# Two queues for q's weights, bias loads further back, w2 in three loads

## The chip, the cores and the metric

The kernel runs on one core of one Trainium2 chip. The metric is the device time of one execution in microseconds (us); for the comparison several executions are timed and their median is taken. Engines go by these names: PE is TensorE's matmul, PEld its weight load, DVE is VectorE, ACT ScalarE, POOL GpSimd, SP SyncE. A "q" behind a name (SPq, ACTq) is the part of that engine that issues DMAs.

## The reference, cut to what matters

The program normalizes x (2048 rows of 640, bf16), feeds the result into an attention branch and an MLP branch, and adds both to x.

```python
def _A_ref(x, wqkv, wo):                 # H = 32 heads, W = 8 taps, dilation 2
    qkv = (x @ wqkv).reshape(B, S, 3, H, Dh)...
    q, k, v = qkv[0], qkv[1], qkv[2]
    idx = pos[:, None] - off[None, :]    # each row sees itself and 7 earlier rows, 2 apart
    logits = jnp.einsum("bhsd,bhswd->bhsw", q, kg) * scale     # idx < 0 masked
    o = jnp.einsum("bhsw,bhswd->bhsd", softmax(logits), vg)
    return o.reshape(B, S, D) @ wo

def _B_ref(x, w1, b1, w2, b2):           # F = 1536
    return gelu(x @ w1 + b1) @ w2 + b2

x = A_x
xn = _layernorm(x, axis=-1)
return x + _A_ref(xn, A_wqkv, A_wo) + _B_ref(xn, B_w1, B_b1, B_w2, B_b2)
```

## The kernel before, in words

The 2048 rows are worked on in four chunks of 512 rows, each of four blocks of 128 rows. x lies in SBUF as `x_sb`, 16 blocks wide; the weights lie there whole, with the 640 input channels in five tiles of 128 (`KT`): `wq_sb`, `wk_sb`, `wv_sb`, `w_sb` (w1, and also w2) and `wo`.

Before the main part the loads are issued in the order of the source (lines 131 to 142), as far as each one's own inputs are ready. On SyncE: x block 0 (L126), q's weights (`load_w(0)`, L129), x blocks 2 and 3, k's weights, x blocks 4 to 7, v's weights, and w1 in two loads (L142). On ScalarE: x block 1 (L132), and the two biases into `b_rt`, 12 rows of b1 (L133) and 5 rows of b2 (L134). Block 1's load waits for a small GpSimd memset in `x_sb` (L120), and the bias loads for one in `b_rt` (L121). The loads share a small set of completion counters, taken in turn, so a later load waits until an earlier one that used the same counter has landed; L142 does so.

Everything behind that runs in an order that is written out by hand, the long string `ORDER`: each name stands for a piece of work, and every engine works through its own instructions in that order. These names matter here:

- `st00` (L213, L215) are block 0's mean and variance on VectorE, `sum1`, `neg1` and `sq1` (L225, L229, L232) those of block 1 on ScalarE, `rs00` and `rs01` (L244, L247) the reciprocal deviations of the two blocks on ScalarE.
- `xn00a`, `xn00b`, `xn01b`, `xn01a` (L264) normalize on VectorE, `tp...` (L279) transpose on TensorE into PSUM, `tc...` (L284) copy the result to `xnT`.
- `ga`, `gb2` to `gb4` (L346) are q's 25 matmuls for block 0, by input tile: `ga` takes tiles 0 and 1, `gb2` tile 2, `gb3` and `gb4` tiles 3 and 4. `gd` and `ge` do the same for block 1. `hj...` (L377) are the q, k and v matmuls of the rest of chunk 0.
- `tb` (L453) is one small matmul that transposes the 17 bias rows, and `b1` (L456) copies them to `bT`, which the first GELU reads (L627).
- `wa`, `wb` and the matmuls at L443 in front of the string work on constants alone and write to a bank that nothing reads.
- `qk0...` (L430) are the products of q and k on VectorE. `f1` (L611) is the first MLP product, `t...` (L690) the second with the attention's output product; they read w1 and w2. `ld2` (L153) loads w2, in four loads.

The first names of the string give the order at the start:

```python
pad01 pad02 st00a st00 sum1 rs00 neg1 xn00a sq1 xn00b tp00a wa tp00b tc00a wb rs01 tc00b ga xn01b gb2 xn01a tp01b
st03a tp01a tb tc01b gb3 tc01a gb4 st03 gd gc0 st02a ge rs03 st02 hj101 xn03 rs02 gc1 xn02 tp03 gc4 st12a tp02 tc03
```

Of the kernel before, what the change touches and what calls it, by code (L numbers as in the profile page):

```python
# [16 lines left out]
S, D, F, H, W, DIL = 2048, 640, 1536, 32, 8, 2  # L17
P = 128
DH = D // H
PAD = (W - 1) * DIL  # L20
KT, FT = D // P, F // P
# [17 lines left out]

ORDER = """  # L40
pad01 pad02 st00a st00 sum1 rs00 neg1 xn00a sq1 xn00b tp00a wa tp00b tc00a wb rs01 tc00b ga xn01b gb2 xn01a tp01b
st03a tp01a tb tc01b gb3 tc01a gb4 st03 gd gc0 st02a ge rs03 st02 hj101 xn03 rs02 gc1 xn02 tp03 gc4 st12a tp02 tc03
hj100 st13a st13 tc02 st12 hj102 hc101 st11a hj111 hc100 st10a hc102 st11 hj010 st10 hc111 ho b1 rs1 hj112 pk rc1 qk01
hj110 xn13 hc112 hj012 tc13 xn11 hj200 hc010 hc110 tc11 qk00 hj011 hc200 hc012 hj201 hc011 xn10 f10_1 hc201 qk02 tc10
xn12 f10_11 tc12 f10_2 ldx ge0_1 f10_5 qk03 ge0_11 ge0_2 f10_3 ge0_5 f10_0 pad11 ge0_3 pa00 pj103 ge0_0 pj100 pc103
pa01 su20 xp2 pj110 pc100 ld2 pj101 pc110 su22 pb01 pj104 su21 pj102 pc101 su23 pb04 pj114 pc104 ng2 pc102 pj112 ldo
# [27 lines left out]
def kernel(  # L74
# [16 lines left out]
    nc = tc.nc  # L91
# [23 lines left out]
    wqkv = [wts.tile([P, KT, D], BF16, name=f"w{s}_sb") for s in "qkv"]  # L115
# [3 lines left out]
    b_rt = consts.tile([P, P], BF16, name="b_rt")  # L119
    nc.gpsimd.memset(x_sb[:, 1, 0:16], 0.0)  # L120
    nc.gpsimd.memset(b_rt[:], 0.0)  # L121
    wqkv_v = A_wqkv.rearrange("(t p) n -> p t n", p=P)
    w1_v = B_w1.rearrange("(t p) n -> p t n", p=P)

    def load_x(b0, b1):
        nc.sync.dma_start(x_sb[:, b0:b1, :], x_nb[:, b0:b1, :])  # L126

    def load_w(s):
        nc.sync.dma_start(wqkv[s][:], wqkv_v[:, :, s * D : (s + 1) * D])  # L129

    load_x(0, 1)
    nc.scalar.dma_start(x_sb[:, 1, :], x_nb[:, 1, :])  # L132
    nc.scalar.dma_start(b_rt[0:FT, :], B_b1.rearrange("(t p) -> t p", p=P))  # L133
    nc.scalar.dma_start(b_rt[FT : FT + KT, :], B_b2.rearrange("(t p) -> t p", p=P))  # L134
    load_w(0)
    load_x(2, BPC)
    load_w(1)
    load_x(BPC, 2 * BPC)
    load_w(2)
    for c in range(2):  # L140
        cs = slice(c * F // 2, (c + 1) * F // 2)
        nc.sync.dma_start(w1_sb[:, :, cs], w1_v[:, :, cs])  # L142
# [5 lines left out]

    def do_ld2():
        w2_v = B_w2.rearrange("(t p) n -> p t n", p=P)  # L150
        for c in range(4):
            ts = slice(c * FT // 4, (c + 1) * FT // 4)
            nc.sync.dma_start(w2_sb[:, ts, :], w2_v[:, ts, :])  # L153

    def do_ldo():
# [695 lines left out]
```

## Time and profile before

| | |
|---|---|
| median of 3 runs | 205.5 us (205.43 to 206.93) |
| profiled execution | 205.49 us |
| its span in the trace | 203.3 us |
| TensorE busy | 199.4 us, 98% of the span |
| VectorE busy | 185.8 us, 91% |
| ScalarE busy | 129.7 us, 64% |
| moved by DMA | 27.31 MB |

The span is the stretch that the trace covers; the profiled execution's own time is 2.19 us longer. Rows of the timeline give start, length, engine, line, operation, output and inputs, and in brackets how long the engine stood idle ahead of it and what ended that. Rows of the chain give start, length and what it was. Rows of the DMA issues give what was loaded, who issued it, how often, the size of one and the median time from issue to landing. Rows of windows give the stretch, its length, the busy time (and instructions) of PE, PEld, DVE, ACT and POOL, TensorE's granted clock, the share of the DMA engines that was busy, and GB/s. Rows of queues give packets, MB and share; q1 carries SyncE's loads, and q10 those of ScalarE.

### The profile page before, as it was taken

What the parts mean: (1) busy time and instruction counts of PE and PEld (TensorE: products, weight loads), DVE (VectorE), ACT (ScalarE), POOL (GpSimd) and SP (SyncE); (2) the same over time, 40 slices, a digit from 0 to 9 for tenths busy, and PEclk for the clock granted to TensorE, in tenths of its full rate; (3) what the DMA queues carried; (4) which work ended last, traced back from release to release, by engine and by line L of the source; (5) the groups of instructions that cost most, each with busy time, mean ns of one, the idle gap of its engine ahead of it and who ended that gap; (6) DMA issues with size and microseconds to landing.
All of it is one profiled execution on the core that took longest, in us unless ns stands there. A gap on an engine that the chain in (4) does not pass through costs nothing.

```text
span 203.3 us, 2874 instructions
## 1 busy us (share of the span) xinstructions
PE 199.4 (98%) x1100; PEld 105.0 (52%) x1100; DVE 185.8 (91%) x159; ACT 129.7 (64%) x237; POOL 29.5 (14%) x35
## 2 busy tenths in 40 slices
PE   8999999999999999999999999999999999999994
PEld 3899455654454555444444544444444445444552
DVE  2899999899997999999999996999979999999981
ACT  5689979999979897555545437697447990211100
POOL 3000000000000400024202500000202702253420
PEclk9999999999999999999999999999999999999999
DMA  6996399940673681849912890001863898895951
GB/s 204 390 395 208 77 355 336 348 148 3 91 155 89 110 148 22 219 92 163 193 17 52 102 99 5 3 0 15 170 98 69 153 118 147 111 120 90 103 90 64
DMA packets 38430, 27.31 MB, mean 134 GB/s; under 512 B 25106, under 2 KB 34578, under 8 KB 38418
## 3 DMA queue, kind: packets, MB, share of 16 engines
q1 hardware_dynamic: 28016, 20.29, 38.2%
q0 software_dynamic: 10080, 6.56, 26.3%
q10 hardware_dynamic: 322, 0.30, 0.4%
q8 instruction: 8, 0.13, 0.3%
q14 instruction: 4, 0.03, 0.0%
HBM read 10.49 MB, written 4.59 MB: 74 GB/s over the span
## 4 chain that ended last, share of the span: by engine, by line
PE 96%; DMA 2%; SPq 0%; DVE 0%; issue 0%
PE T L690 27%; PE hps L611 25%; PE pps L333 24%; PE lo L646 7%; PE gps L377 7%; DMA wq_sb<-in_A_wqkv_dram 2%; PE hi L646 2%; PE gps L346 1%; PE L L480 1%; PE tp L279 0%; SPq L126 0%; DVE prod L658 0%; PE tb L453 0%
## 5 line engine op out<-in xcount | busy, mean ns | idle before, releaser
L611 PE MATMUL hps<-xnT,w_sb 128*128 128x512 bf16 x240 | 56.9, 379 | 0.0
L430 DVE TENSOR_TENSOR prod<-qT,kT 128x5120 bf16<-128x5120 bf16 x16 | 44.5, 2820 | 0.1
L690 PE MATMUL T<-hT,w_sb 128*128 128x512 bf16 x180 | 43.4, 379 | 0.0
L611 PEld LDWEIGHTS <-w_sb 128*128 128x128 bf16 x240 | 23.5, 98 | 27.5
L702 POOL DMA_DIRECT2D out_dram<-x_sb x15 | 20.9, 1492 | 87.5 <-DMA x_sb<-x_sb 87.5
L627 ACT ACTIVATE hT<-hps,bT 128x512 bf16<-128x512 f32 x36 | 23.9, 689 | 12.1 <-PE hps L611 9.6
L690 PEld LDWEIGHTS <-w_sb 128*128 128x128 bf16 x180 | 17.5, 98 | 21.1 <-issue 0.4
L693 ACT ACTIVATE x_sb<-T,bT 128x512 bf16<-128x512 f32 x15 | 10.3, 688 | 25.6 <-PE T L690 24.5
L581 DVE TENSOR_TENSOR prod<-vT,ax 128x5120 bf16<-128x5120 bf16 x8 | 22.4, 2820 | 2.7 <-PE L L480 1.5
L581 DVE TENSOR_TENSOR prod<-vT,x_sb 128x5120 bf16<-128x5120 bf16 x8 | 22.2, 2817 | 0.0
L592 POOL DMA_DIRECT2D prod<-prod x6 | 7.8, 1300 | 77.5 <-DVE prod L581 77.5
L170 ACT ACT_TABLE_LOAD x14 | 18.0, 1283 | 1.0 <-PEq L835 0.7
L471 DVE TENSOR_TENSOR prod<-prod 128x4096 bf16<-128x4096 bf16 x8 | 18.3, 2291 | 0.3
L333 PE MATMUL pps<-xnT,wv_sb 128*128 128x512 bf16 x75 | 18.5, 379 | 0.0
L690 PE MATMUL T<-oT,wo 128*128 128x512 bf16 x75 | 18.5, 379 | 0.0
L333 PE MATMUL pps<-xnT,wq_sb 128*128 128x512 bf16 x75 | 18.1, 379 | 0.0
L465 DVE TENSOR_TENSOR prod<-prod 128x4096 bf16<-128x4096 bf16 x8 | 18.0, 2286 | 0.0
L333 PE MATMUL pps<-xnT,wk_sb 128*128 128x512 bf16 x75 | 18.0, 380 | 0.0
L594 DVE TENSOR_TENSOR prod<-prod 128x2560 bf16<-128x2560 bf16 x10 | 14.8, 1487 | 0.1
L333 PEld LDWEIGHTS <-wq_sb 128*128 128x128 bf16 x75 | 8.8, 117 | 7.5
L333 PEld LDWEIGHTS <-wv_sb 128*128 128x128 bf16 x75 | 8.7, 118 | 7.6 <-issue 0.4
L333 PEld LDWEIGHTS <-wk_sb 128*128 128x128 bf16 x75 | 8.6, 118 | 7.7 <-issue 0.8
(91 smaller groups left out, 242.6 us busy)
## 6 DMA issues: line engine op xcount, KB each, us to landing
prod<-prod POOLq DMA_DIRECT2D x6, 640.0 KB, 6.8
ax<-attn SPq DMA_DIRECT2D x8, 256.0 KB, 3.9
x_sb<-attn SPq DMA_DIRECT2D x8, 256.0 KB, 4.5
w_sb<-in_B_w_dram SPq DMA_DIRECT2D x2, 960.0 KB, 11.0
out_dram<-x_sb SPq DMA_DIRECT2D x3, 640.0 KB, 6.8
w_sb<-in_B_w_dram SPq DMA_DIRECT2D x4, 480.0 KB, 6.6
out_dram<-x_sb POOLq DMA_DIRECT2D x15, 128.0 KB, 5.6
x_sb<-in_A_x_dram SPq DMA_DIRECT2D x2, 640.0 KB, 7.0
```

The lines of the kernel that those rows point to most:

```text
L170: nc.scalar.preload_act_table_set(name)
L333: nc.tensor.matmul(ps[:], lhsT=wqkv_p[which][:, ti, to, :], rhs=xnT[:, ti, :], start=(ti == 0), stop=(ti == KT - 1),)
L430: nc.vector.tensor_tensor(out=prod[:, j], in0=q[:, :, at].unsqueeze(1).to_broadcast([P, W, KT, P]), in1=window(k, at), op=ALU.mult,)
L465: nc.vector.tensor_tensor(out=low, in0=low, in1=high, op=ALU.add)
L471: nc.vector.tensor_tensor(out=first, in0=first, in1=rows[:, :, t * P : (t + 1) * P], op=ALU.add)
L581: nc.vector.tensor_tensor(out=prod[:, j], in0=window(qkv_tile(n, 2), slice(j * P, (j + 1) * P)), in1=ax_view(n)[:, j, :, :].unsqueeze(2).t ...
L594: nc.vector.tensor_tensor(out=low, in0=low, in1=high, op=ALU.add)
L611: nc.tensor.matmul(ps[:], lhsT=w1_sb[:, ti, ft * P : (ft + 1) * P], rhs=tiles["xnT", n][:, ti, :], start=(ti == 0), stop=(ti == KT - 1),)
L627: nc.scalar.activation(hT, tiles["hps", n, ft][:], ACT.Gelu_apprx_tanh, bias=bT[:, ft : ft + 1], scale=1.0)
L646: nc.tensor.matmul(out_ps(bl, hi), lhsT=lhs, rhs=rhs[:, CH:D] if hi else rhs[:, 0:CH], start=pc == 0 and k == 0, stop=pc == 4 and k == len ...
L690: nc.tensor.matmul(ps[:], lhsT=lhs, rhs=rhs, start=pc == 0 and k == 0, stop=pc == 4 and k == len(srcs) - 1)
L702: nc.gpsimd.dma_start(dst, src, accum_op=ALU.add)
```

## The change

q's weights are loaded in two pieces: input tiles 0 to 2 by SyncE, in the place of the whole load, and tiles 3 and 4 by ScalarE. The two bias loads go from ScalarE to SyncE, behind v's weights and ahead of w1. In the order by hand, `tb` goes from the start to a place ahead of `b1`. w2 is loaded in three loads of four tiles in place of four loads of three.

```diff
 ORDER = """
...
-st03a tp01a tb tc01b gb3 tc01a gb4 st03 gd gc0 st02a ge rs03 st02 hj101 xn03 rs02 gc1 xn02 tp03 gc4 st12a tp02 tc03
-hj100 st13a st13 tc02 st12 hj102 hc101 st11a hj111 hc100 st10a hc102 st11 hj010 st10 hc111 ho b1 rs1 hj112 pk rc1 qk01
+st03a tp01a tc01b gb3 tc01a gb4 st03 gd gc0 st02a ge rs03 st02 hj101 xn03 rs02 gc1 xn02 tp03 gc4 st12a tp02 tc03 hj100
+st13a st13 tc02 st12 hj102 hc101 st11a hj111 hc100 st10a hc102 st11 hj010 st10 hc111 ho tb b1 rs1 hj112 pk rc1 qk01
...
     load_x(0, 1)
     nc.scalar.dma_start(x_sb[:, 1, :], x_nb[:, 1, :])
-    nc.scalar.dma_start(b_rt[0:FT, :], B_b1.rearrange("(t p) -> t p", p=P))
-    nc.scalar.dma_start(b_rt[FT : FT + KT, :], B_b2.rearrange("(t p) -> t p", p=P))
-    load_w(0)
+    for queue, a, b in ((nc.sync, 0, 3), (nc.scalar, 3, KT)):
+        queue.dma_start(wqkv[0][:, a:b, :], wqkv_v[:, a:b, 0:D])
     load_x(2, BPC)
     load_w(1)
     load_x(BPC, 2 * BPC)
     load_w(2)
+    nc.sync.dma_start(b_rt[0:FT, :], B_b1.rearrange("(t p) -> t p", p=P))
+    nc.sync.dma_start(b_rt[FT : FT + KT, :], B_b2.rearrange("(t p) -> t p", p=P))
...
     def do_ld2():
         w2_v = B_w2.rearrange("(t p) n -> p t n", p=P)
-        for c in range(4):
-            ts = slice(c * FT // 4, (c + 1) * FT // 4)
+        for c in range(3):
+            ts = slice(c * FT // 3, (c + 1) * FT // 3)
             nc.sync.dma_start(w2_sb[:, ts, :], w2_v[:, ts, :])
```

In the built program before, ScalarE starts with a table load (L170), then issues block 1's load, b1 and b2. In the built program after, it issues the piece of q's weights first, then block 1's load, and then comes the table load.

## Prediction

> **What bounds the kernel now.** I read the busy table first, then the chain that ended last, cut to the first 14 us (the change acts there), then the timeline of those microseconds, and last the DMA queues in small windows.
>
> ```profile
> PE 199.4 (98%) x1100; PEld 105.0 (52%) x1100; DVE 185.8 (91%) x159; ACT 129.7 (64%) x237; POOL 29.5 (14%) x35
> PE 96%; DMA 2%; SPq 0%; DVE 0%; issue 0%
> 6.30:20.00 13.70, 13.69 (x157) 13.58 (x158) 12.44 (x29) 10.91 (x27) 0.00 (x0) 1.00 0.94 334
> 1.19 5.07 DMA wq_sb<-in_A_wqkv_dram
> 6.27 0.05 issue
> 6.31 1.03 PE gps L346 x15
> ```
>
> TensorE is busy for 98% and carries 96% of the chain; from 6.3 to 20 us it works 13.69 of 13.70 us, and the chain that leads into it is q's weights, landing at 1.19 + 5.07 = 6.26 us. So TensorE in program order is the bound, with no holes behind the start: any later start of the first q matmul (L346, 6.31 us) goes into the end one to one, and any earlier start can help only as far as that matmul's other inputs allow. Those come from this chain on ScalarE and VectorE:
>
> ```profile
> 0.88 0.38 ACTq L132 DMA_DIRECT2D x_sb<-in_A_x_dram  x1
> 3.65 0.74 ACT L225 ACTIVATE trash<-x_sb 128x640 bf16<-128x640 bf16 x1 [1.63 <-DMA x_sb<-in_A_x_dram]
> 4.50 0.29 ACT L244 ACTIVATE logv<-mv,eps_t 128x1 f32<-128x1 f32 x1
> 4.83 0.20 ACT L247 ACTIVATE rstd<-logv 128x1 f32<-128x1 f32 x1
> 5.07 0.63 DVE L264 TENSOR_SCALAR xn<-x_sb,mv,rstd 128x256 bf16<-128x256 bf16 x2 [0.66 <-ACT rstd L247]
> 5.47 0.28 PE L279 MATMUL tp<-ident,xn 128*128 128x128 bf16 x2 [0.26 <-DVE xn L264]
> 5.79 0.70 DVE L284 COPY xnT<-tp 128x256 bf16<-128x256 bf16 x2
> 6.67 0.64 DVE L264 TENSOR_SCALAR xn<-x_sb,neg,rstd 128x384 bf16<-128x384 bf16 x2 [0.18 <-ACT rstd L247]
> 7.18 0.47 PE L279 MATMUL tp<-ident,xn 128*128 128x128 bf16 x5
> ```
>
> ScalarE works in program order: sum1 of block 1 (L225) stands ahead of rs00 (L244, L247), the rstd of block 0. So block 1's load (L132, landed 0.88 + 2.7 = 3.58) holds block 0's normalization too, and then every step to the first q matmul. The first of the two copies at 5.79 (0.70 for both) ends near 6.14: xnT is ready 0.17 us ahead of the matmul at 6.31. That 0.17 is all that faster weights could bring.
>
> **The change part by part.** *q's weights.* In the instruction order of the built kernel ScalarE's queue issues the two-tile piece of q first and block 1's load second, because that load waits for a memset of x_sb (L120) and the weights wait for nothing; the table load comes third. So the change doesn't only split a load: it puts 2 x 128 x 1280 B = 328 KB in front of the 164 KB that the chain above waits for. Is a queue served in order, and how do two queues share?
>
> ```profile
> wq_sb<-in_A_wqkv_dram SPq DMA_DIRECT2D x1, 800.0 KB, 5.1
> x_sb<-in_A_x_dram SPq DMA_DIRECT2D x1, 320.0 KB, 5.4
> wk_sb<-in_A_wqkv_dram SPq DMA_DIRECT2D x1, 800.0 KB, 7.0
> x_sb<-in_A_x_dram SPq DMA_DIRECT2D x1, 640.0 KB, 8.1
> wv_sb<-in_A_wqkv_dram SPq DMA_DIRECT2D x1, 800.0 KB, 9.3
> q1 hardware_dynamic: 144, 0.16, 59.4%
> q10 hardware_dynamic: 143, 0.16, 45.3%
> 0.00:3.00 3.00, 2.22 (x6) 0.87 (x7) 0.00 (x0) 1.28 (x1) 1.53 (x13) 1.00 0.38 109
> 3.00:4.10 1.10, 1.10 (x4) 0.32 (x3) 0.83 (x2) 0.45 (x1) 0.00 (x0) 1.00 0.92 297
> 4.10:4.94 0.84, 0.84 (x5) 0.37 (x4) 0.27 (x2) 0.78 (x5) 0.00 (x0) 1.00 1.06 392
> 4.94:5.37 0.43, 0.27 (x4) 0.09 (x2) 0.30 (x2) 0.40 (x3) 0.00 (x0) 1.00 1.07 393
> ```
>
> The first five rows are times from issue to landing; with the issues of SyncE (1.19, 1.66, 2.23, 2.74, 3.65 us) they land at 6.26, 7.06, 9.23, 10.84 and 12.95, in the order of issue. The next two are packets of SyncE's queue (q1) and ScalarE's (q10) from 2.3 to 3.3 us, while both had work: 144 against 143, equal shares. The last four give bytes: 3.00 x 109 + 1.10 x 297 = 654 KB moved by 4.10 us, 983 KB by 4.94, 1152 KB by 5.37.
>
> q's weights whole need x block 0, block 1 and all of q: 164 + 164 + 819 = 1147 KB, moved by 5.37, landed by 6.26, 0.89 later. After the change the same 1147 KB stand in front of SyncE's last q byte, now on two queues: its three tiles land at about 6.26 again. Gain nothing, at most the 0.17.
>
> Block 1's load: with equal shares ScalarE's queue has moved its 328 + 164 = 492 KB when SyncE's has moved 492 KB too, 984 KB in all: 4.94 us by the table. From the last byte to the landing it is 0.58 (block 1 now: 328 KB with block 0 at 3.00, landed 3.58) to 0.89 (q), so 5.5 to 5.8; but the table holds a dip (297 GB/s from 3.00 to 4.10, in which ScalarE's queue moved the small bias rows) that goes with the change, and at 392 those 1.1 us would be 0.27 shorter: 5.25 to 5.55. I take 5.35, nearer the row of this same load. Bounds: at the earliest ScalarE's queue is served first and block 0 beside it, 656 KB: 4.10 less the dip's 0.27 and plus 0.58 gives 4.4; at the latest SyncE's is served 5 to 3, 984 + 328 = 1312 KB: 4.94 + 328/393 = 5.77, plus 0.7 gives 6.47.
>
> So sum1 starts at 5.42 in place of 3.65, and rs00, the transposes, rs01 and block 1's xn all move with it by 1.77. The first q matmul could start at 6.14 + 1.77 = 7.91, against 6.31: 1.60 late. Its successors agree: block 1's xn (6.67) moves by 1.77 to end its first part near 8.75, where TensorE is done with the 15 matmuls (7.91 + 0.87). What TensorE loses there is given back nowhere, since the 13.69 of 13.70 us behind it are its own work. Bounds by the same step: 4.4 gives 0.65 late, 6.47 gives 2.7.
>
> A rule of the Trainium skill bears on the aim of the edit. "DMA: Bandwidth & Descriptors", section "Issuing engines are not separate DMA queues", says that loads issued by different engines run on the same 16 DMA engines and interleave, so that a second issuer saves only the issuing time. By it the split would be worth 0 and not even the 0.17; the 144 against 143 packets agree.
>
> *Bias loads behind v's weights, tb moved.* SyncE's two bias issues (0.64 and 0.27 us where ScalarE makes them now) come between v's issue, which ends at 4.50, and w1's first, which waits for q until 6.28 as now.
>
> ```profile
> 1.31 0.64 ACTq L133 DMA_DIRECT2D b_rt<-in_B_b_dram  x1
> 1.98 0.27 ACTq L134 DMA_DIRECT2D b_rt<-in_B_b_dram  x1
> 6.28 2.23 SPq L142 DMA_DIRECT2D w_sb<-in_B_w_dram  x2
> 7.65 0.01 PE tb L453
> 13.86 1.26 PE L377 MATMUL gps<-xnT,wq_sb 128*128 128x256 bf16 x10
> 15.05 0.17 DVE L456 COPY bT<-tb 128x17 f32<-128x17 f32 x1
> 20.49 3.83 PE L611 MATMUL hps<-xnT,w_sb 128*128 128x512 bf16 x17
> ```
>
> The biases now land just behind v, near 13.0. tb stands behind the ten matmuls of 13.86, at about 14.95 now and 16.5 after: 3.5 us of cover, cost 0 (it takes 0.01 of the chain in either place). Without the cover TensorE would stand at tb, and behind VectorE's b1 (L456) wait the first four q k products. w1 keeps its issue time and lands by about 18.7 (6.7 + 12.0, the larger of its two landings), against 20.49 + 1.6: more cover than now. Should the bias issues push it by all 0.91, it is still 19.6. Range of this part 0 to 0.
>
> *w2 in three loads.* One issue fewer, so the landings that later loads wait for keep their places.
>
> ```profile
> 28.27 3.12 SPq L153 DMA_DIRECT2D w_sb<-in_B_w_dram  x4
> w_sb<-in_B_w_dram SPq DMA_DIRECT2D x4, 480.0 KB, 6.6
> 50.82 1.29 PE T L690 x6
> ```
>
> All issued by 31.39, landed by about 38, first used at 50.82: 12 us of cover, cost 0; a third larger piece adds perhaps 2 us to a landing.
>
> **Sum.** The profiled execution took 205.49 us (span 203.3, 2.19 around it); the median of the runs shown is 205.5, so no correction. 205.49 + 1.60 = **207.1**. Own range, from landings between 4.6 and 5.95 us: 206.3 to 207.7.
>
> **The rivals.** *ScalarE's queue is served first.* For it: in its busiest part that queue took nearly all of the rate, and SyncE's second load was slow to begin; against it the equal count over the whole microsecond. It gives 205.49 + 0.65 = 206.1.
>
> *SyncE's queue gets more*, 5 to 3 as in the bound: 205.49 + 2.7 = 208.2. For it: SyncE has more and earlier issues; against it the same count.
>
> *TensorE runs slow again.* Its first matmuls ran at half the later rate:
>
> ```profile
> 0.78 4.43 PE L443 MATMUL idle<-const-bfloat16-1.0 128*128 128x512 bf16 x13 [0.78 <-PEq L835]
> 25.83 1.29 PE hps L611 x6
> ```
>
> Ten of 512 and three of 128 columns took 4.43 us; at 1.29/6 = 0.215 us for 512 they would take 2.3. The change opens a hole from 5.21, where these end, to the transposes at 5.47 + 1.77 = 7.24, and only eight small matmuls up to 7.91. If TensorE falls back and repeats the slow stretch, that is another 2.1 us: 209.2. Against it: in this trace it never falls back, though with no hole over 0.3 us to try it. The granted clock reads 1.00 in the slow stretch too, so that column can't show it. The Trainium skill, "TensorE: Matmul & The Clock Gate", section "What's actually happening", has the array fall to half after an idle window of about 3.4 us; by it a hole of 2.0 us is too short, though the few matmuls behind it leave some doubt, and no run here shows it.
>
> *Not slower.* Block 1's load isn't held by the weights in front of it, because the early rate (109 GB/s over the first 3 us) has room that a second full queue fills. The point from which it decides: a landing by 3.73 us; then the first q matmul starts when xnT is ready, 0.17 earlier than now, 205.3. Against it: 656 KB would have to be moved by 3.15 us, where the chip had moved 327 KB by 3.00 with both queues at work. This is also the case in which the change would do what it says.
>
> **How the numbers follow.** Forecast 0.57; ScalarE first 0.13; SyncE more 0.10; slow TensorE 0.12; not slower 0.05; a gain that I don't see 0.03. A measurement of this kernel can tell about 1%, 2.06 us, from no change: the limit is 207.56. Slower: 0.12 + 0.10 + the upper sixth of the forecast (0.09) = 0.31; within: 0.48 + 0.13 + 0.05 = 0.66; faster 0.03. The range 205.9 to 208.2 leaves out slow TensorE, not slower and the gain: 0.20.
>
> **What would show it.** Right: block 1's load lands at 4.6 to 5.95 us, sum1 starts just behind it, the first q matmul at 7.2 to 8.5 waits for xnT and no longer for wq_sb; SyncE's q tiles land near 6.3; TensorE has a hole from 5.2 us; tb near 16.5 with no wait; from the first k matmul on everything is later by one constant. Wrong: a first q matmul that waits for wq_sb still, block 1 landed before 4.4, six 512-column matmuls that take more than 1.29 us after the hole, or TensorE idle at tb.

## The result, and the profile after

| | median of runs | lowest to highest | ratio to before |
|---|---|---|---|
| before | 205.63 us | 205.22 to 208.37 | |
| changed | 208.48 us | 207.02 to 210.16 | 1.0114, 95% interval 1.0078 to 1.0151 |

The changed kernel is slower by 1.1%. Its six runs fall into groups by the clock that TensorE was granted: 207.02 and 207.19 us at a mean clock of 1.00, 208.48, 208.48 and 208.60 at 0.991 to 0.992, and 210.16 at 0.984. The last is the profiled execution (span 208.1 us), so this trace holds both losses in their largest form. One run of the first group alone would have looked like the forecast. Ratios leave out a run that is over 1.5% above the fastest of its kernel, so a median may move by more than its ratio.

First the page of the changed kernel: busy time by engine, granted clock in 40 slices of 5.2 us, and the chain that ended last.

```profile
PE 201.3 (97%) x1100; PEld 107.5 (52%) x1100; DVE 185.9 (89%) x159; ACT 129.7 (62%) x237; POOL 29.5 (14%) x35
...
PEclk9669999999999999999999999999999999999999
...
PE 95%; DMA 2%; issue 0%; DVE 0%; ACT 0%; POOL 0%; POOLq 0%
```

TensorE has 1.9 us more busy time for the same 1100 instructions, and the clock row shows where: second and third slice, nowhere else. Now the timeline of the first 20 us (issues of ScalarE's queue, then ScalarE, then TensorE).

```profile
0.74 0.46 ACTq L134 DMA_DIRECT2D wq_sb<-in_A_wqkv_dram  x1
1.24 0.48 ACTq L132 DMA_DIRECT2D x_sb<-in_A_x_dram  x1
...
6.38 0.74 ACT L226 ACTIVATE trash<-x_sb 128x640 bf16<-128x640 bf16 x1 [3.34 <-DMA x_sb<-in_A_x_dram]
...
8.06 0.39 PE L280 MATMUL tp<-ident,xn 128*128 128x128 bf16 x2 [3.31 <-DVE xn L265]
...
8.89 1.81 PE L347 MATMUL gps<-xnT,wq_sb 128*128 128x128 bf16 x15
...
11.02 3.57 PE L347 MATMUL gps<-xnT,wq_sb 128*128 128x128 bf16 x35
14.43 1.25 PE L378 MATMUL gps<-xnT,wk_sb 128*128 128x256 bf16 x10
...
19.90 0.17 PE L454 MATMUL tb<-ident,b_rt 128*128 128x17 bf16 x1
```

The piece of q is issued at 0.74, block 1 at 1.24, behind it. sum1 starts at 6.38, where it started at 3.65 before, and waits 3.34 us for block 1 alone. Everything behind it is late: TensorE's transposes come after a hole of 3.31 us, the first q matmul stands at 8.89 (6.31 before), and what it waits for is xn, not the weights. That is 2.58 us. Then the q matmuls themselves: 15 take 1.81 us and 35 take 3.57, against 1.03 and 2.13 before. The rows of before that follow the first 15:

```profile
7.51 2.13 PE L346 MATMUL gps<-xnT,wq_sb 128*128 128x128 bf16 x35
9.48 1.25 PE L377 MATMUL gps<-xnT,wk_sb 128*128 128x256 bf16 x10
```

Windows of the trace of the changed kernel (columns as before: stretch, length, busy time of PE, PEld, DVE, ACT and POOL, granted clock, DMA share, GB/s):

```profile
7.27:14.03 6.76, 5.97 (x57) 5.92 (x58) 4.86 (x15) 3.79 (x13) 0.00 (x0) 0.50 1.06 396
14.03:20.00 5.97, 5.97 (x66) 5.95 (x65) 4.24 (x14) 4.37 (x11) 0.00 (x0) 1.00 0.56 209
20.00:200.00 180.00, 180.00 (x929) 91.07 (x928) 172.40 (x122) 119.40 (x212) 27.94 (x22) 1.00 0.61 115
```

All through these 6.76 us the granted clock is 0.50, and behind them it is 1.00. From 20 us on TensorE is busy without a gap, 180.00 of 180.00 us. From the first q matmul to the first k matmul it takes 5.54 us (8.89 to 14.43); in a run that starts late and whose clock held it takes 3.31 (shown below), and before it took 3.17 (6.31 to 9.48). Against the run with 3.31, 2.58 us from a late start and 2.23 from the clock make 4.81, and the span grew by 208.1 - 203.3 = 4.8. The 0.14 us between 3.17 and 3.31 stands in neither term and about as much is made up later: in the run with 3.31 the first w1 matmul starts 1.74 us later than before, the last matmuls 1.63 later. So the two terms hold the difference to within some 0.15 us, and the experiments take them apart.

### The profile page after: what moved, and what is told of

Its sections match the earlier page's. It is cut to its first block, busy times and chain, and to the rows that moved or that the text cites. A ratio compares the mean times of both kernels' runs of the same rounds, so it can differ in the third digit from the quotient of the medians.

```text
span 208.1 us, 2873 instructions
## 1 busy us (share of the span) xinstructions
PE 201.3 (97%) x1100; PEld 107.5 (52%) x1100; DVE 185.9 (89%) x159; ACT 129.7 (62%) x237; POOL 29.5 (14%) x35
## 4 chain that ended last, share of the span: by engine, by line
PE 95%; DMA 2%; issue 0%; DVE 0%; ACT 0%; POOL 0%; POOLq 0%
PE T L691 26%; PE hps L612 25%; PE pps L334 24%; PE lo L647 7%; PE gps L378 7%; DMA x_sb<-in_A_x_dram 2%; PE gps L347 2%; PE hi L647 2%; PE L L481 1%; PE tp L280 1%; DVE xn L265 0%; PE idle L444 0%; DVE prod L659 0%; ACT rstd L248 0%; ACT trash L226 0%
```

## The experiments

The theory: block 1's load stands behind q's piece in ScalarE's queue, so TensorE starts late; the hole that this opens then makes the clock fall. The rivals: the two queues slow each other whatever the order; the bias loads or w2 cost something; the fall has nothing to do with the hole.

### The split kept, block 1 issued first

```diff
+    nc.gpsimd.memset(wqkv[0][:, 3, 0:16], 0.0)
```

With a memset of its own to wait for, q's piece is issued behind block 1.

> The changed kernel, but ScalarE's piece of q's weights waits for a memset behind the one that x block 1's load waits for, so block 1's load is issued first and the piece second; the split into two queues, the bias loads, tb and w2 stay as changed. Theory (the loss comes from block 1's load standing behind the weights in ScalarE's queue): block 1 lands near 3.6 us again, the first q matmul at 6.1 to 6.4, no hole in TensorE over 0.5 us, span 203.1 to 203.5, time 205.3 to 205.7. Rival (two queues for q's weights cost by themselves, since both pieces are later): the first q matmul waits for wq_sb and starts at 7 us or later, 206.2 or more.

Measured: 205.64 us, ratio 1.0007 [0.9987, 1.0028], no run with a fallen clock among 12. Its timeline:

```profile
0.88 0.38 ACTq L133 DMA_DIRECT2D x_sb<-in_A_x_dram  x1
1.30 0.45 ACTq L135 DMA_DIRECT2D wq_sb<-in_A_wqkv_dram  x1
...
3.78 0.74 ACT L227 ACTIVATE trash<-x_sb 128x640 bf16<-128x640 bf16 x1 [1.76 <-DMA x_sb<-in_A_x_dram]
...
6.55 1.07 PE L348 MATMUL gps<-xnT,wq_sb 128*128 128x128 bf16 x15
```

The whole loss is gone with the order of two issues. The first q matmul is at 6.55, a little later than I expected; its weight load waits 0.17 us for wq_sb, as the one before waited 0.28, so the split didn't bring q's weights earlier. So two queues do no harm by themselves, and bring no earlier start either: block 1 lands in time, and the first q matmul comes no sooner.

### q's weights whole, bias loads and w2 as changed

```diff
-    for queue, a, b in ((nc.sync, 0, 3), (nc.scalar, 3, KT)):
-        queue.dma_start(wqkv[0][:, a:b, :], wqkv_v[:, a:b, 0:D])
+    load_w(0)
```

> The bias loads on SyncE behind v's weights, tb moved, w2 in three loads; q's weights whole on SyncE as before. Theory: nothing, 205.3 to 205.7, first q matmul at 6.3. Rival (tb or w1 waits now): TensorE idle ahead of tb or of the first w1 matmul, 206 or more.

Measured: 205.34 us, 0.9996 [0.9983, 1.0010], first q matmul at 6.29 us. The other two edits cost nothing that can be measured.

### The hole filled: too much, then as needed

```diff
-WARM = 10
+WARM = 20      (first try)
+WARM = 15      (second try)
```

WARM sets how many 512-column matmuls on constants TensorE does ahead of the first transposes. They fill the hole and leave all else as changed.

> The changed kernel with 20 in place of 10 constant matmuls of 512 columns at the start, so that TensorE is busy to about 7.2 us. Theory (two losses: the late start, and a clock that falls to half after the hole): the late start stays, the granted clock reads 1.00 from 6 to 20 us in every run, every run ends near 207.1 (span 205.0 to 205.7), and the runs at 208.5 and above vanish. Rival (all of the loss is late data): the spread of 207.0 to 210.2 stays. Second rival (the added matmuls are themselves in the way): 207.5 or more in all runs, with the first transposes waiting for TensorE.

Measured with 20: 207.30 us (207.07 to 207.53), 1.0080 [1.0067, 1.0093], the clock 1.0 in all six runs. But the filler ran to 8.14 us and so stood in the way of the transposes, whose xn was ready near 7.3: a clean test of the clock, not of the late start. So a second try was sized to end where they begin.

> The changed kernel with 15 in place of 10 constant matmuls, so that TensorE is busy to about 6.9 us, just ahead of the transposes. Theory (late start plus a clock that falls in the hole): no run with a granted clock under 0.997, all runs at 206.7 to 207.3, and no later than with 20 matmuls, which ended at 8.1 us and stood 0.8 us in the way of the transposes. Rival (20 matmuls were needed because the clock looks back over the whole stretch up to 8 us): some runs at 208.4 or above again.

Measured with 15: 207.05 us (206.96 to 207.24), 1.0061 [1.0035, 1.0086], the clock at least 0.999 in all 12 runs. Its timeline:

```profile
0.78 6.05 PE L444 MATMUL idle<-const-bfloat16-1.0 128*128 128x512 bf16 x18 [0.78 <-PEq L836]
5.60 0.74 ACT L226 ACTIVATE trash<-x_sb 128x640 bf16<-128x640 bf16 x1 [2.56 <-DMA x_sb<-in_A_x_dram]
...
7.29 0.28 PE L280 MATMUL tp<-ident,xn 128*128 128x128 bf16 x2 [0.46 <-DVE xn L265]
...
7.95 1.00 PE L347 MATMUL gps<-xnT,wq_sb 128*128 128x128 bf16 x15
...
9.30 2.12 PE L347 MATMUL gps<-xnT,wq_sb 128*128 128x128 bf16 x35
11.26 1.26 PE L378 MATMUL gps<-xnT,wk_sb 128*128 128x256 bf16 x10
```

The start is as late as the change makes it (7.95, 1.64 late), and its span of 204.9 us is 1.6 over that of before: here is the first loss alone, 1:1. From the first q matmul to the first k matmul it takes 3.31 us. With the hole down to 0.46 us the clock held in every run, with 20 matmuls too (0 of 18 runs in all), while it fell in 9 of 12 runs of the changed kernel. So in this kernel the second loss hangs on the hole.

### The changed kernel again

No edit; the same kernel measured a second time, beside the fillers.

> The changed kernel once more, for the spread of its runs. Theory: three groups, one clock window of half speed apart: near 207.1 with a granted clock of 1.00, near 208.5 with 0.992, near 210.1 with 0.984. Rival (one broad spread of late data): times between the groups, with no tie to the granted clock.

Measured: 208.45 us, 1.0109 [1.0066, 1.0152]; one run of 207.21 at clock 1.00, five from 208.07 to 208.58 at 0.991 to 0.992, and none of the third group this time. The profiled one took 208.55. Timeline and windows:

```profile
5.78 0.74 ACT L226 ACTIVATE trash<-x_sb 128x640 bf16<-128x640 bf16 x1 [2.74 <-DMA x_sb<-in_A_x_dram]
6.51 0.28 ACT L245 ACTIVATE logv<-mv,eps_t 128x1 f32<-128x1 f32 x1
...
7.46 0.28 PE L280 MATMUL tp<-ident,xn 128*128 128x128 bf16 x2 [2.01 <-DVE xn L265]
...
8.13 1.31 PE L347 MATMUL gps<-xnT,wq_sb 128*128 128x128 bf16 x15
...
9.77 3.22 PE L347 MATMUL gps<-xnT,wq_sb 128*128 128x128 bf16 x35
12.82 1.25 PE L378 MATMUL gps<-xnT,wk_sb 128*128 128x256 bf16 x10
```

```profile
0.00:3.00 3.00, 2.22 (x6) 0.87 (x7) 0.00 (x0) 1.24 (x1) 1.53 (x13) 1.00 0.35 79
3.00:4.10 1.10, 1.10 (x4) 0.32 (x3) 0.80 (x2) 0.04 (x1) 0.00 (x0) 1.00 1.09 383
4.10:4.94 0.84, 0.84 (x3) 0.30 (x2) 0.29 (x2) 0.00 (x0) 0.00 (x0) 1.00 1.03 375
...
5.25:8.66 3.41, 1.40 (x21) 1.06 (x20) 1.28 (x4) 2.73 (x9) 0.00 (x0) 1.00 1.06 392
8.66:12.07 3.41, 3.41 (x36) 3.41 (x34) 2.95 (x10) 1.54 (x5) 0.00 (x0) 0.50 1.07 395
12.07:14.00 1.93, 1.93 (x28) 1.92 (x26) 1.86 (x5) 1.26 (x4) 0.00 (x0) 1.00 1.06 399
```

The first q matmul is 1.82 late. Then the clock is at half for 3.41 us, between 8.66 and 12.07, and from 8.13 to 12.82 TensorE needs 4.69 us where 3.31 do at full clock: 1.38 lost. Together 3.20, and the span grew by 206.5 - 203.3 = 3.2. One such stretch of 3.41 us at half in a span of 206.5 makes a mean clock of 0.992, two make 0.983: the clocks of the runs (0.991 to 0.992, and 0.984) count the stretches.

### A smaller piece on ScalarE

```diff
-    for queue, a, b in ((nc.sync, 0, 3), (nc.scalar, 3, KT)):
+    for queue, a, b in ((nc.sync, 0, 4), (nc.scalar, 4, KT)):
```

> The changed kernel with four tiles of q's weights on SyncE and one on ScalarE, so 164 KB in place of 328 KB ahead of x block 1. Theory (bytes ahead of block 1, shared in equal parts by the queues): 656 KB in place of 984 KB until block 1 is moved, at 393 GB/s 0.83 us less: block 1 lands at 4.4 to 5.5, the first q matmul 0.7 to 1.8 us later than before, time 206.2 to 207.0, no fall of the clock since the hole is under 2.5 us. Rival (the place in the queue costs by itself, whatever the size): block 1 lands at 5.3 to 6.4 as with two tiles.

Measured: 205.86 us, 1.0044 [1.0013, 1.0075]: the time lies under my 206.2 to 207.0, and the clock fell in some runs. In the profiled run block 1 still landed late, and sum1 with it:

```profile
5.35 0.74 ACT L226 ACTIVATE trash<-x_sb 128x640 bf16<-128x640 bf16 x1 [2.40 <-DMA x_sb<-in_A_x_dram]
...
7.03 0.28 PE L280 MATMUL tp<-ident,xn 128*128 128x128 bf16 x2 [1.51 <-DVE xn L265]
...
7.70 1.00 PE L347 MATMUL gps<-xnT,wq_sb 128*128 128x128 bf16 x15
```

Block 1's landing, at 1.18 + 4.1 = 5.3 us, lies inside the theory's 4.4 to 5.5 and at the edge of the rival's 5.3 to 6.4, so this trace doesn't tell the two apart. The profiled run took 206.74; the other seven runs in which the clock held took 205.58 to 205.97, hardly more than before, so there the load must mostly have landed earlier than in this trace, and earlier than either theory had it (a trace of such a run isn't at hand; why stays open). And in 4 of 12 runs the clock fell (0.990 to 0.992, 207.83 to 208.77), where I had expected none. Those four are 2 to 3 us slower than the seven, and 3.41 us at half clock can cost 1.71 at most, so they must have started later too; how long the hole was in them isn't known.

### The late load without a second queue

The kernel of before, with block 1's load moved to SyncE's queue behind q whole.

```diff
-    nc.scalar.dma_start(x_sb[:, 1, :], x_nb[:, 1, :])
     load_w(0)
+    nc.sync.dma_start(x_sb[:, 1, :], x_nb[:, 1, :])
```

> The kernel before with x block 1 loaded by SyncE behind q's whole weights; nothing is split, bias, tb and w2 are as before. Theory (what counts is the bytes ahead of block 1): 1147 KB must be moved first, block 1 lands at 6.0 to 6.4, the first q matmul at 8.6 to 9.0, 207.8 to 208.3 where the clock holds, and 209.3 or above where it falls in a hole of 3 us, in at least half of the runs. Rival (two queues at work are what delays block 1): block 1 lands by 5 us and the time is 206.8 or less.

Measured: 209.85 us (209.03 to 210.47), 1.0185 [1.0142, 1.0228]. The trace:

```profile
6.51 0.74 ACT L225 ACTIVATE trash<-x_sb 128x640 bf16<-128x640 bf16 x1 [4.50 <-DMA x_sb<-in_A_x_dram]
...
8.20 0.29 PE L279 MATMUL tp<-ident,xn 128*128 128x128 bf16 x2 [2.68 <-DVE xn L264]
```

One queue, a later load, a bigger loss: what counts here is what stands ahead of block 1, and a second queue isn't needed for it. The first q matmul came at 8.87, as the theory has it. The size of the time was missed: the clock fell in four of six runs (0.984 to 0.992), and the two runs whose clock held still took 209.89 and 210.24. Of those two no trace was taken, and why they were slow stays open.

### rs00 ahead of sum1

```diff
-pad01 pad02 st00a st00 sum1 rs00 neg1 ...
+pad01 pad02 st00a st00 rs00 sum1 neg1 ...
```

The changed kernel, with block 0's normalization no longer behind the step that waits for block 1.

> The changed kernel with rs00 ahead of sum1 in ScalarE's order, so that block 0's normalization no longer stands behind the wait for block 1. Theory (both chains hang on block 1, each moved by about the same): the first q matmul returns to 6.3 to 7.1 us, but TensorE then waits for block 1's transposes, which come only 0.3 us earlier than in the changed kernel (rs00's place in front of sq1 is gone): 206.5 to 206.9 instead of 207.1; the hole is split in two parts of under 1.5 us, so the clock reads 0.997 or more in every run. Rival (only block 0's chain was held up): 205.8 or less.

Measured: 206.74 us (206.50 to 207.24), 1.0049 [1.0022, 1.0075], the clock at least 0.998 in all 12 runs. As the theory has it, the lateness moves to the next one that needs block 1:

```profile
6.19 1.17 PE L347 MATMUL gps<-xnT,wq_sb 128*128 128x128 bf16 x15
8.83 0.54 PE L280 MATMUL tp<-ident,xn 128*128 128x128 bf16 x5 [1.47 <-DVE xn L265]
```

The first 15 q matmuls run at 6.19, no later than before, so q's weights are there; then TensorE waits 1.47 us for block 1's xn. This is better than the change by itself but gives back only 0.2 to 0.3 us of its late start (207.05 to 206.74, and 205.59 to 205.45 for the kernel of before beside each) and saves the fall of the clock.

### Three tries for a faster version

q in two loads, both on SyncE, tiles 0 and 1 first: once with block 1's memset taken out (its load waits for nothing), once with the memset kept. And, as a control, q whole with the memset taken out.

```diff
-    nc.gpsimd.memset(x_sb[:, 1, 0:16], 0.0)       (first and third)
...
-    for queue, a, b in ((nc.sync, 0, 3), (nc.scalar, 3, KT)):
+    for queue, a, b in ((nc.sync, 0, 2), (nc.sync, 2, KT)):   (first and second)
+    load_w(0)                                     (third, in place of the loop)
```

> A try for a better version: block 1 alone on ScalarE's queue and without the memset that holds it back, q's weights on SyncE in two loads, tiles 0 and 1 first (328 KB), then tiles 2 to 4; bias, tb and w2 as changed. Theory: block 1 lands 0.1 earlier, tiles 0 and 1 land at about 5 us, so the first q matmul waits for xnT alone and starts at 6.0 to 6.15, 0.15 to 0.3 us earlier than before: 205.0 to 205.3. Rival (the third tile becomes the wait, as 1147 KB still stand ahead of q's last byte, landing near 6.3, where TensorE needs it at 6.4 to 6.7): no gain, 205.4 or more.

> q's weights on SyncE in two loads, tiles 0 and 1 and then 2 to 4, block 1's load on ScalarE with its memset, bias, tb and w2 as changed. Theory 1 (the split in one queue costs): 206.1 or more, q's second load lands at 7 us or later and TensorE waits for it. Theory 2 (the earlier issue of block 1 costs): 205.2 to 205.6, second load landed by 6.4.

> q's weights whole on SyncE, bias, tb and w2 as changed, and block 1's load on ScalarE without the memset that holds it back; to find which part of the try with tiles 0 and 1 first cost 1 us. Theory 1 (the split of q's weights into two loads of one queue slows the rate behind it): no loss here, 205.2 to 205.6. Theory 2 (block 1's load, issued 0.14 us earlier at the same moment as block 0's, delays block 0 or all that follows): 206.1 or more here.

Measured: 206.59 us, 1.0043 [1.0017, 1.0069]; 206.24 us, 1.0030 [1.0004, 1.0057]; and 205.50 us, 1.0017 [0.9976, 1.0058]. The split loads lose a little in both forms. Without the memset the first q matmul came at 6.51, not at the 6.0 to 6.15 of my theory, and TensorE then waited 1.03 us for the second load. With the memset kept it starts a little earlier than before and waits 0.33 us; the timeline of that kernel, and beneath it the window from 4 to 7 us of the same kernel, of the third and of before:

```profile
5.97 0.72 PE L347 MATMUL gps<-xnT,wq_sb 128*128 128x128 bf16 x10
7.02 0.47 PE L347 MATMUL gps<-xnT,wq_sb 128*128 128x128 bf16 x5 [0.33 <-DMA wq_sb<-in_A_wqkv_dram]
```

```profile
4.00:7.00 3.00, 2.38 (x24) 1.49 (x22) 1.98 (x7) 2.32 (x9) 0.00 (x0) 1.00 0.96 305
```

```profile
4.00:7.00 3.00, 2.56 (x14) 1.28 (x12) 1.96 (x8) 2.53 (x9) 0.00 (x0) 1.00 1.04 370
```

```profile
4.00:7.00 3.00, 2.64 (x26) 1.60 (x25) 1.98 (x8) 2.49 (x9) 0.00 (x0) 1.00 1.06 385
```

With q in two loads the rate in those 3 us is 305 GB/s (248 without the memset), with q whole 370 and 385, each from one trace. The control's clock fell in 3 of its 12 runs (208.10 to 209.00 us). So the earlier first tiles are paid for by later last ones. Why the rate falls stays open. No version beat the kernel of before.

## Why the prediction was right, and where not

The direction and the first cause held: block 1's load stands behind q's piece, and where the clock held the changed kernel took 207.02 to 207.21 us, as forecast. The size held only in part. The median of 208.48 lies 1.4 us over the point of 207.1 and above both the range of 205.9 to 208.2 and my own, because a rival that I gave 0.12 came true in most runs. The ratio of 1.0114, put on 205.49, gives 207.8 and lies inside the wider range; as it mixes runs with and without the fall of the clock, that is luck and no merit of the sum.

*The bound.* Right: in the changed kernel too TensorE is busy 180.00 of 180.00 us from 20 us on, and in three traces the growth of the span is the lateness of the start plus the loss by the clock, 4.81 for 4.8, 3.20 for 3.2 and 1.64 for 1.6. My "given back nowhere" is right to about 0.1 us (1.74 late at the first w1 matmul, 1.63 at the last ones, with 15 fillers).

*The order in ScalarE's queue.* Right, and shown by the kernel that only turns it round (1.0007). The rule of the Trainium skill, "DMA: Bandwidth & Descriptors", section "Issuing engines are not separate DMA queues", agrees with that kernel: the split by itself bought nothing.

*q's three tiles on SyncE.* Right in the main: they landed at 6.1 us with 15 fillers, at 1.19 + 5.1 = 6.29 in the second measurement and at 1.20 + 5.9 = 7.1 in the profiled run of the result, against 6.26 for the whole load. In the changed kernel they were never waited for.

*Block 1's landing.* The term was sized a little low: 5.35 forecast, 5.55 with the filler, 5.75 in the second measurement and 6.35 in the profiled run of the result, the first two inside my own range, the last only inside the wide bounds. Equal shares held over the whole; packets and MB of the two queues in the second measurement of the changed kernel up to 5.1 us:

```profile
q1 hardware_dynamic: 447, 0.55, 35.7%
...
q10 hardware_dynamic: 401, 0.48, 28.5%
```

My evidence for them was weak, though: within the microsecond of 144 to 143 packets it was 69 to 26 from 2.3 to 2.6 us and 17 to 81 from 2.6 to 2.9. In the changed kernel too they held only as a sum: in the second measurement ScalarE's queue had 56 packets to SyncE's 144 in the first 3 us, then 153 to none up to 3.5 us. The 6.35 is a late tail: in that trace 403 of ScalarE's 416 packets came by 5.25 us, the last three after 5.75.

What failed is the credit of 0.27 us for the dip. The dip did go (383 GB/s from 3.00 to 4.10 us, 297 before), but the first 3 us were slower by as much: 79 GB/s against 109. By 4.10 us 3.00 x 79 + 1.10 x 383 = 658 KB were moved, against 654 before. Without the credit my table gave 5.5 to 5.8, where two of the three landings lie.

*From sum1 to the first q matmul.* The steps held, with a small error that went the other way: rs00 follows sum1's start by 0.73 us (5.78 to 6.51) and not by 0.85 (before, block 0's statistics on VectorE, done at 4.40, stood close ahead of it). So a start of sum1 that is 2.13 later made the first q matmul 1.82 later: 0.12 less by this, and the 0.17 of waiting for weights less. That is why the late start alone came to 1.64 and 207.05 us, hardly off 1.60 and 207.1: in part luck, as the late landing and these smaller terms cancel. The successors agreed too: with rs00 first, block 1's xn still held TensorE for 1.47 us.

*Biases, tb and w2.* Right, 0: tb runs at 19.90 and 18.30 us without a wait, and those edits alone measured 0.9996. One step in it was wrong without harm: w1 didn't keep its issue time. The first bias issue took 2.82 us in the profiled run (from 4.55, to just behind the landing of q's tiles), so w1's first came at 7.73 in place of 6.28, more than the 0.91 I had allowed; its first matmul at 25.39 still waited for nothing.

*TensorE runs slow again.* This step failed, twice. Its chance: I held a hole of 2.0 us for too short, and the clock fell in 9 of the 12 runs of the changed kernel (four of six, five of six). Its price: I took the slow stretch at the start, 2.1 us, where one stretch of 3.41 us at half cost 1.38 us and the two of the profiled execution 2.23. So the likeliest time was 207.05 + 1.4 = 208.45, where the second measurement's median lies. The rule of the Trainium skill that I leaned on ("TensorE: Matmul & The Clock Gate", "What's actually happening") has its length confirmed by the 3.41 us, but not its condition: the 3.41 us ahead of the fall, 5.25 to 8.66, have TensorE busy for 1.40, so that no idle stretch of that length was needed. I had also written that the granted clock can't show it; it can, for the fall (0.50), though it reads 1.00 in the slow stretch at the start.

*The other rivals.* ScalarE's queue was not served first, SyncE's got only slightly more (447 packets to 401), and block 1 was held by what stood in front of it.

The traces show more of the condition. From the end of the slow start on, each records the granted clock in stretches of 3.41 us or whole multiples of it, and where these begin differs from run to run: at 3.8 to 6.8 us in the 13 traces. The first such stretch of the profiled run of the result, which a fall follows, then of the smaller piece on ScalarE and of rs00 first, which none follows:

```profile
3.82:7.23 3.41, 0.94 (x7) 0.40 (x5) 0.84 (x3) 0.85 (x3) 0.00 (x0) 1.00 1.04 383
```

```profile
5.47:8.88 3.41, 1.90 (x27) 1.53 (x26) 1.93 (x7) 2.60 (x9) 0.00 (x0) 1.00 1.07 395
```

```profile
6.55:9.96 3.41, 1.94 (x33) 1.71 (x32) 1.59 (x6) 2.21 (x8) 0.00 (x0) 1.00 1.05 385
```

TensorE is busy for 0.94 us of the first, 1.90 and 1.94 of the others. Over all 13 traces the clock falls 14 times (11 of them at the end, where the work runs out), each time behind a stretch with TensorE busy for 1.40 us or less, and never behind one with 1.84 or more. So what decides seems to be how much of the hole lies in one stretch, and that depends on where the stretches begin in that run. This was read from the traces afterwards; no run was made to test it.

What stays open: where in a run the stretches begin, and how long the hole was in the fallen runs that left no trace.

## What to carry to other kernels

Before moving a load to another engine's queue, read in the built order what it will stand ahead of there: 328 KB in front of a 164 KB load that a chain waits for cost 1.6 us or more, while the split by itself bought nothing. Price a late start of the bounding engine twice, once for the lateness and once for what the hole does to its clock (here 1.4 us more in most runs), and fill the hole with work of the right length to tell the two apart.

## What the runs showed of the hardware

The fall of TensorE's clock comes in whole stretches of 3.41 us at 0.50 and leaves no trace but the clock: the matmuls of that stretch just take longer. In the 13 traces it came behind stretches of that length in which TensorE was busy for 1.40 us or less, and never behind one with 1.84 or more. It isn't special to the changed kernel: of the 81 executions of the kernel before that ran beside these, 8 had a mean clock below 0.995 and took 208.0 to 210.4 us. Six of them had one such stretch, which can cost 1.71 us at most, but were 2.5 to 3.4 us over the median, so they must have lost time by something else too, perhaps a late load that opened a hole; none of the eight left a trace. And two loads in one queue, for the same bytes in the same order, moved 305 GB/s from 4 to 7 us where one load moved 370 to 385, in one trace each; the cause is open.
